# A gated feed-forward kernel: both raw products of the next unit placed ahead of a unit's last product, and the third weight sums of unit 1 moved to GpSimd

## The chip, the cores and the metric

The kernel runs on one core of a Trainium2 chip. The metric is device time in microseconds (us) of one execution; lower is better. The kernel before takes 542.69 us (median of 3 runs, 542.49 to 542.69).

Engine names as in the profile: PE is TensorE (matmul), PEld its weight loads, DVE is VectorE, ACT is ScalarE, POOL is GpSimd, SP issues DMAs.

## The reference

```python
# x: 2048 x 1024, w_gate and w_up: 1024 x 3584, w_down: 3584 x 1024, all bf16
def reference(x, w_gate, w_up, w_down):
    g = jnp.einsum("bsd,df->bsf", x, w_gate)
    u = jnp.einsum("bsd,df->bsf", x, w_up)
    h = jax.nn.gelu(g, approximate=True) * u
    return jnp.einsum("bsf,fd->bsd", h, w_down)
```

## The kernel before

The kernel multiplies 2 x 2 blocks with seven products in place of eight (a Strassen-like scheme). The rows are handled in two passes; in each pass there are 14 units, one for each 256 columns of the gate and up weights, followed by the down projection. A unit makes seven products for gate and for up, so each product is eight matmuls of 128 x 128 weights by 512 columns. Two of the seven use the bf16 inputs as they are: the raw products. The other five use sums of blocks (`s` of weights, `t` of inputs), which are kept in fp32. Unit 0 of the first pass is computed in the plain way, and unit 1 is made while the engines are still busy with that.

This is the part of a unit that the argument needs. `e`, `c` and `d` are pairs of PSUM banks, where the matmuls put their results; `hT` holds the products of gelu(gate) and up, the input of the down projection; `snap` copies a bank out with ScalarE; `keep` makes combinations of the down weights, by a ScalarE copy into a bank of the `c` pair and a VectorE subtraction, and is used only in units 2 to 13 of the first pass.

```python
def product(ps, lhs, rhs, start):
    for k in range(KH):                       # KH = 4
        matmul(ps, lhs[:, k, :], rhs[k], start and k == 0, k == KH - 1)

def first_product(e, xT, w):                  # raw (bf16)
    for i in range(2):
        product(e[i], w[:, i, :KH, :P], [xT[0][:, k, :] for k in range(KH)], True)
    return [snap(e[i], "p1") for i in range(2)]

def unit(u, banks, xT, w, s, t, p1, after_p5, aside, keep, ahead_of_p4, snap_first):
    ...
    e, c, d = banks
    for i in GU: product(c[i], w[:, i, KH:, :P], b21, True)       # second raw product
    g, up = add(c, p1)                                            # VectorE: two sums
    for i in GU: product(e[i], s["s2"][i], t["t2"], False)
    keep(0, c[0])
    g = gelu(g); times(2 * u, 0, g, up)
    u2 = [snap(e[i], "u2") for i in GU]
    keep(1, c[0]); keep(2, c[1])
    c = d
    for i in GU: product(c[i], s["s1"][i], t["t1"], True)
    p5 = [snap(c[i], "p5") for i in GU]
    after_p5()                                                    # GpSimd: next unit's s1..s4
    for i in GU: product(e[i], s["s3"][i], t["t3"], False)
    ...                                                           # sums with p5
    for i in GU: product(c[i], s["s4"][i], t["tb"], False)        # "fourth sum's product"
    ...
    ahead_of_p4()                                                 # first_product of unit u + 1
    for i in GU: product(e[i], s["sa"][i], t["t4"], False)        # last product
    times(2 * u, 1, gelu(g), up)
    times(2 * u + 1, 0, gelu(e[0]), e[1])                         # last hT multiply
# [some lines joined; branches for unit 1 and calls of `aside`, which inserts other work, cut]

def keep_part(j, part, ps):
    ...
    nc.scalar.copy(out=ps, in_=a)
    dve(made[j][:, part], ps, b, SUB)
```

Ahead of the loop, VectorE makes the weight sums of unit 1:

```python
    finish(bank[0:4], 0)
    s["s1"] += s["how"]["s1"](s, range(1, 2))
    nxt = {"p1": first_product(odd, xT, w)}
    s.make("sa", "s2", "s3", "s4")
    t.make("t1")
```

Of the kernel before, what the change touches and what calls it, by code (L numbers as in the profile page):

```python
# [10 lines left out]
def kernel(  # L11
# [26 lines left out]
    P = nc.NUM_PARTITIONS  # L38
# [13 lines left out]
    KH = NKB // 2  # L52
# [29 lines left out]
    def slot(shape, dtype, name):  # L82
        return kpool.tile(shape, dtype, name=name, tag="k")
# [3 lines left out]
    even, odd, cc, dd = bank[6:8], bank[0:2], bank[2:4], bank[4:6]  # L87
# [17 lines left out]
    def snap(ps, name):  # L105
        t = slot([P, N], f32, name)
        nc.scalar.copy(out=t, in_=ps)  # L107
        return t
# [40 lines left out]
    def sums_s(w, eng):  # L149
        GU = range(2)  # L150
        sh = [P, KH, P]
        a11, a21 = [[w[:, i, :KH, h : h + P] for i in GU] for h in (0, P)]
        a12, a22 = [[w[:, i, KH:, h : h + P] for i in GU] for h in (0, P)]
        return Sums(
            how={
                "s1": lambda q, GU=GU: [new(eng, a21[i], a22[i], ADD, "s1", sh) for i in GU],
                "s2": lambda q: [new(eng, q["s1"][i], a11[i], SUB, "s2", sh) for i in GU],
                "s3": lambda q: [new(eng, a11[i], a21[i], SUB, "s3", sh) for i in GU],
                "s4": lambda q: [new(eng, a12[i], q["s2"][i], SUB, "s4", sh) for i in GU],
                "sa": lambda q: [cast(a22[i], "sa", sh) for i in GU],  # L160
            }
        )
# [22 lines left out]
    def product(ps, lhs, rhs, start):  # L185
        for k in range(KH):
            matmul(ps, lhs[:, k, :], rhs[k], start and k == 0, k == KH - 1)

    def first_product(e, xT, w):
        for i in range(2):  # L190
            product(e[i], w[:, i, :KH, :P], [xT[0][:, k, :] for k in range(KH)], True)
        return [snap(e[i], "p1") for i in range(2)]

    def unit(u, banks, xT, w, s, t, p1, after_p5, aside, keep, ahead_of_p4, snap_first):
        GU = range(2)

        def add(ps, other):

            g = new(dve, ps[0], other[0], ADD, "sum", dtype=f32)
            dve(ps[1], ps[1], other[1], ADD)  # L200
            return g, ps[1]

        b21 = [xT[0][:, KH + k, :] for k in range(KH)]
        e, c, d = banks
        for i in GU:
            product(c[i], w[:, i, KH:, :P], b21, True)
        aside(-2)
        g, up = add(c, p1)
        aside(-1)
        for i in GU:  # L210
            product(e[i], s["s2"][i], t["t2"], False)
        aside(0)
        keep(0, c[0])
        if snap_first:
            u2 = [snap(e[i], "u2") for i in GU]
            g = gelu(g)
        else:
            g = gelu(g)
        c11 = g, up
        if not snap_first:  # L220
            times(2 * u, 0, *c11)
            u2 = [snap(e[i], "u2") for i in GU]
        keep(1, c[0])
        keep(2, c[1])
        c = d
        for i in GU:
            product(c[i], s["s1"][i], t["t1"], True)
        p5 = [snap(c[i], "p5") for i in GU]
        after_p5()
        for i in GU:  # L230
            product(e[i], s["s3"][i], t["t3"], False)
        g, up = new(dve, e[0], p5[0], ADD, "sum", dtype=f32), banks[1][not snap_first]
        dve(up, e[1], p5[1], ADD)
        if snap_first:
            times(2 * u, 0, *c11)
        for i in GU:
            product(c[i], s["s4"][i], t["tb"], False)
        times(2 * u + 1, 1, gelu(g), up)
        aside(1)
        g, up = add(c, u2)  # L240
        ahead_of_p4()
        for i in GU:
            product(e[i], s["sa"][i], t["t4"], False)
        times(2 * u, 1, gelu(g), up)
        aside(2)
        times(2 * u + 1, 0, gelu(e[0]), e[1])
# [106 lines left out]
    sa = {}  # L353
# [113 lines left out]
    xT = new_x()  # L467
# [4 lines left out]
    w = load_w(1)  # L472
# [4 lines left out]
    def plain(ps, c, kos, parts=1):  # L477
        n = N // parts
        for k in range(kos.start, kos.stop, 2):
            for part in range(parts):  # L480
                cols = slice(part * n, (part + 1) * n)
                for p, (j, i) in zip(ps, [(j, i) for j in range(2) for i in range(2)]):
                    for ko in (k, k + 1):
                        matmul(
                            p[:, cols],
                            wf[:, i, ko, j * P : (j + 1) * P],
                            xT[c][:, ko, cols],
                            ko == 0 and part == 0,
                            ko == NKB - 1,
                        )  # L490
# [6 lines left out]
    s, t = sums_s(w, dve), sums_t(xT)  # L497
    with tc.manual_schedule(engines={ENG.Activation}):
        def keep_warm(n, cols):
            for _ in range(n):  # L500
                nc.tensor.matmul(  # L501
                    bank[3][:, :cols], lhsT=warm[:, :P], rhs=warm[:, :cols], start=True, stop=True
                )

        keep_warm(NWARM, N)
        for i in range(NS):
            if i > 0:
                keep_warm(3, 2 * P)
            turn(xT, xn0, 0, i, on_act if i == 1 else on_dve)
        plain(bank[0:4], 0, range(0, 2), parts=2)  # L510
        plain(bank[0:4], 0, range(2, NKB))
        s["s1"] = s["how"]["s1"](s, range(1))
        finish(bank[0:4], 0)
        s["s1"] += s["how"]["s1"](s, range(1, 2))
        nxt = {"p1": first_product(odd, xT, w)}
        s.make("sa", "s2", "s3", "s4")
        t.make("t1")

    seen = xpool.tile([P, 1], f32, name="seen")
# [15 lines left out]
    for ip in range(NPASS):  # L535
        for u in range(1 if ip == 0 else 0, NU):
            js = making(u) if ip == 0 else []

            def prepare():
                nonlocal ahead  # L540
                if first:
                    pool_behind(t["t4"][-1])
                nxt["w"], nxt["s"] = ahead, None
                if u + 1 < NU:
                    nxt["s"] = make_s(ahead, pool)
                if u + 2 < NU:
                    ahead = load_w(u + 2)
                if len(js) == 1:
                    store_made(js[0])
                for j in js[1:]:  # L550
                    keep_whole(j)
                if ip == 0:
                    fetch_wd(making(u + 1))

            def keep(part, ps):
                if js:
                    keep_part(js[0], part, ps)

            def aside(part):
                if (ip, u) == (0, 1) and part < 0:  # L560
                    rest_of_0(part + 2)
                if part == 0 and "t4" not in t:
                    t.make("t4")

            def ahead_of_p4():
                if u + 1 < NU:
                    nxt["p1"] = first_product(even if u % 2 else odd, xT, nxt["w"])

            e = odd if u % 2 else even
            p1 = nxt.pop("p1", None) or first_product(e, xT, w)  # L570
            first = (ip, u) == (0, 1)
            with tc.manual_schedule(engines={ENG.Activation}) if first else nullcontext():
                unit(u, (e, cc, dd), xT, w, s, t, p1, prepare, aside, keep, ahead_of_p4, first)
            if u + 1 < NU:
                w, s = nxt["w"], nxt["s"]

        last = ip == NPASS - 1
        got, nxt = {}, {}

        def more(step):  # L580

            nonlocal ahead
            if last:
                return
            if step in (-1, 0, 2):
                store_made({-1: NJ - 3, 0: NJ - 2, 2: NJ - 1}[step])
            if step == 0:
                xT[:] = new_x()
            if step >= 24 and step % 2 == 0 and step // 2 - 12 < len(moves):
                c, ko = moves[step // 2 - 12]  # L590
                transposing(xT, c, ko, (2 * (ip + 1) + c) * N)
            if step == 50:
                got["w"], ahead = load_w(0), load_w(1)
            if step == 58:
                got["s"] = make_s(got["w"], dve)
            if step == 62:
                got["t"] = make_t(xT)

        down(ip, even + cc, dd + odd, last, more)
        even, odd, cc, dd = odd, even, dd, cc  # L600
        if not last:
            w, t, s = got["w"], got["t"], got["s"]
# [29 lines left out]
```

## Time and profile before

| quantity | before | where it is read |
|---|---|---|
| time, median of 3 | 542.69 us | the runs |
| span | 540.6 us | head of the page |
| PE busy | 535.9 us, 99% | page, part 1 |
| one unit, from unit 2 on | 12.60 us | starts of the fourth sum's product, timeline |
| end of the plain products to unit 1's fourth sum (end of that product's first matmul) | 6.11 us | matmul ends in the trace |

The page of the kernel before, three of its parts: engines with busy time and share, the chain that ended last, and four groups of PE (line, operation, output<-inputs, shape, count | busy us, mean ns of one | idle before).

```profile
PE 535.9 (99%) x2414; PEld 378.8 (70%) x2414; DVE 341.4 (63%) x526; ACT 258.7 (48%) x463; POOL 236.4 (44%) x213
...
PE bank L111 98%; PE bank L501 1%; PE bank L448 0%; ACT st L412 0%; DVE warm L432 0%
...
L111 PE MATMUL bank<-t,s 128*128 128x512 f32 x648 | 157.4, 398 | 0.0
...
L111 PE MATMUL bank<-xT,w 128*128 128x512 bf16 (+1 forms) x504 | 116.2, 377 | 0.0
...
L111 PE MATMUL bank<-t,sa 128*128 128x512 f32 x216 | 58.6, 413 | 0.0
...
L111 PE MATMUL bank<-tb,s 128*128 128x512 f32 x216 | 53.3, 389 | 0.0
```

TensorE is the limit, and it is almost always fed. The group names tell the products: `xT,w` raw, `t,s` the three from sums of both sides, `tb,s` the fourth sum's, `t,sa` the last. Their means differ although all do the same size: 389 ns where an fp32 product follows another, 413 ns for the last product, which stands between two raw ones. Matmuls overlap, so these means are not the time that each adds; for that one compares the ends of consecutive matmuls. The Trainium skill, "Perfetto Trace Analysis", section on the tensor engine instruction, says that these ends are computed from the instruction's size, not observed. A single distance is therefore modelled; summed over a unit, the distances agree with the starts (12.60 us from 319.66 to 332.26 below).

The order of the products in one unit of the second pass, from the timeline of PE of the kernel before (start us, length us, instructions):

```profile
319.66 1.98 PE L111 MATMUL bank<-tb,s 128*128 128x512 f32 x8
321.48 1.90 PE L111 MATMUL bank<-xT,w 128*128 128x512 bf16 x8
323.03 2.19 PE L111 MATMUL bank<-t,sa 128*128 128x512 f32 x8
325.06 1.90 PE L111 MATMUL bank<-xT,w 128*128 128x512 bf16 x8
326.61 5.82 PE L111 MATMUL bank<-t,s 128*128 128x512 f32 x24
332.26 1.98 PE L111 MATMUL bank<-tb,s 128*128 128x512 f32 x8
```

Type changes twice each way per unit. From 319.66 to 332.26 is 12.60 us. The distance in ns of each matmul's end from the end of the one before, in that unit, worked out from the trace:

```
tb,s  227 227 226 227 227 226 227 226
xT,w  232 215 216 216 216 216 215 216
t,sa  228 226 230 236 227 234 231 226
xT,w  232 215 216 216 216 216 215 216
t,s   228 226 230 235 228 234 231 227 226 227 227 226 ... (then 227, 227, 226 to the end)
```

A bf16 matmul adds 215.7 ns, an fp32 one 226.6. The first bf16 matmul after fp32 adds 232, and the first eight fp32 matmuls after bf16 add about 25 ns too much together.

The list of PEld's waits of the kernel before (who waited <- for what: us in all, times, longest). "issue" means no producer was found:

```profile
PEld L111 <- issue: 14.0, 53, 0.3
...
PEld bank L111 <- DVE t L90: 0.3, 1, 0.3
PEld bank L111 <- DVE hT L90: 0.3, 1, 0.3
```

The 53 waits are the changes from fp32 to bf16. The two waits for VectorE are the only real stalls after the start, both in unit 1.

### The profile page before, as it was taken

The numbers are of one execution on the slowest core, as the hardware profiler recorded it, in microseconds if no ns is written. First come the engines' busy times: TensorE is split into PE (matmuls) and PEld (weight loads), VectorE is DVE, ScalarE is ACT, GpSimd is POOL, SyncE is SP. The second block draws the span as 40 slices with busy tenths as digits, with TensorE's granted clock in tenths as the row PEclk, the third lists the DMA queues.
The fourth block names the chain that finished last, engine by engine and source line by source line (L and its number), as shares of the span: only waits on it lengthen the run. The fifth ranks groups of instructions, "written<-read, shape, count | busy, mean of one in ns | idle before, by whom it ended". The sixth has DMA issues, their size and how long they took to land.

```text
span 540.6 us, 7439 instructions
## 1 busy us (share of the span) xinstructions
PE 535.9 (99%) x2414; PEld 378.8 (70%) x2414; DVE 341.4 (63%) x526; ACT 258.7 (48%) x463; POOL 236.4 (44%) x213
## 2 busy tenths in 40 slices
PE   9999999999999999999999999999999999999997
PEld 5567777667766646888876776677777775488885
DVE  2986666776666895694945545555544559676730
ACT  2566666566665410255355555555555541114431
POOL 0069966677774400000097777777766600000000
PEclk9999999999999999999999999999999999999999
DMA  9776666666654899979672222222331069363751
GB/s 245 152 187 176 175 183 203 190 185 199 200 165 171 269 381 313 295 189 294 230 194 79 78 79 78 79 78 80 84 100 50 1 196 384 140 236 95 231 188 49
DMA packets 108133, 93.28 MB, mean 173 GB/s; under 512 B 17216, under 2 KB 92992, under 8 KB 108096
## 3 DMA queue, kind: packets, MB, share of 16 engines
q1 hardware_dynamic: 108096, 92.82, 59.2%
q8 instruction: 19, 0.31, 0.3%
q14 instruction: 18, 0.15, 0.1%
HBM read 74.45 MB, written 15.20 MB: 166 GB/s over the span
## 4 chain that ended last, share of the span: by engine, by line
PE 99%; ACT 0%; DVE 0%; issue 0%
PE bank L111 98%; PE bank L501 1%; PE bank L448 0%; ACT st L412 0%; DVE warm L432 0%
## 5 line engine op out<-in xcount | busy, mean ns | idle before, releaser
L93 POOL TENSOR_TENSOR s<-w 128x512 fp32r<-128x512 bf16 x100 | 116.9, 1189 | 154.9 <-PE bank L111 154.9
L111 PE MATMUL bank<-t,s 128*128 128x512 f32 x648 | 157.4, 398 | 0.0
L111 PEld LDWEIGHTS bank<-t,s 128*128 128x128 f32 x648 | 121.6, 188 | 28.2 <-DVE t L90 0.3
L111 PE MATMUL bank<-xT,w 128*128 128x512 bf16 (+1 forms) x504 | 116.2, 377 | 0.0
L107 ACT COPY p<-bank 128x512 f32<-128x512 f32 x124 | 70.5, 591 | 94.0 <-PE bank L111 94.0
L90 DVE TENSOR_TENSOR hT<-g,bank 128x512 bf16<-128x512 f32 x112 | 76.6, 687 | 55.1 <-ACT g L179 49.5
L111 PEld LDWEIGHTS <-w 128*128 128x128 bf16 x504 | 45.1, 98 | 59.0 <-issue 13.4
L90 DVE TENSOR_TENSOR sum<-bank,p 128x512 f32<-128x512 f32 x54 | 37.4, 692 | 52.6 <-PE bank L111 50.9
L179 ACT ACTIVATE g<-sum 128x512 f32<-128x512 f32 x81 | 51.5, 636 | 34.5 <-DVE sum L90 33.6
L111 PE MATMUL bank<-q 128*128 128x512 f32 x240 | 58.9, 389 | 0.0
L111 PE MATMUL bank<-t,sa 128*128 128x512 f32 x216 | 58.6, 413 | 0.0
L93 POOL TENSOR_TENSOR s<-w,s 128x512 fp32r<-128x512 bf16 x50 | 57.7, 1175 | 0.0
L93 POOL TENSOR_TENSOR s<-s,w 128x512 fp32r<-128x512 f32 x50 | 57.0, 1161 | 0.0
L111 PE MATMUL bank<-tb,s 128*128 128x512 f32 x216 | 53.3, 389 | 0.0
L111 PEld LDWEIGHTS bank<-q 128*128 128x128 f32 x240 | 45.1, 188 | 9.3
L111 PE MATMUL bank<-raw,hT 128*128 128x512 bf16 x224 | 48.7, 379 | 0.0
L111 PEld LDWEIGHTS bank<-t,sa 128*128 128x128 f32 x216 | 40.7, 188 | 10.6
L111 PEld LDWEIGHTS bank<-tb,s 128*128 128x128 f32 x216 | 40.6, 188 | 8.4
L102 ACT CAST tb<-raw 128x512 fp32r<-128x512 bf16 x28 | 17.2, 626 | 59.6 <-DMA raw<-in_w_down_dram 24.2
L107 ACT COPY u<-bank 128x512 f32<-128x512 f32 x62 | 35.9, 590 | 19.7 <-PE bank L111 19.7
L90 DVE TENSOR_TENSOR bank<-bank,p 128x512 f32<-128x512 f32 x54 | 37.8, 700 | 8.9 <-PE bank L111 5.8
L90 DVE TENSOR_TENSOR q<-hT 128x512 fp32r<-128x512 bf16 x56 | 38.5, 687 | 4.7 <-PE bank L111 4.7
(45 smaller groups left out, 444.7 us busy)
## 6 DMA issues: line engine op xcount, KB each, us to landing
raw<-in_w_down_dram SPq DMA_DIRECT2D x80, 256.0 KB, 4.8
q<-td SPq DMA_DIRECT2D x60, 256.0 KB, 5.0
w<-in_w_gate_dram SPq DMA_DIRECT2D x27, 512.0 KB, 5.9
w<-in_w_up_dram SPq DMA_DIRECT2D x27, 512.0 KB, 7.0
td<-m SPq DMA_DIRECT2D x12, 768.0 KB, 4.6
w<-td SPq DMA_DIRECT2D x6, 1024.0 KB, 9.5
out_dram<-st SPq DMA_DIRECT2D x32, 128.0 KB, 1.7
td<-w SPq DMA_DIRECT2D x2, 768.0 KB, 7.0
```

The costliest lines, as they stand in the source:

```text
L90: nc.vector.tensor_tensor(out=out, in0=a, in1=b, op=op)
L93: nc.gpsimd.tensor_tensor(out=out, in0=a, in1=b, op=op)
L102: nc.scalar.copy(out=t, in_=src)
L107: nc.scalar.copy(out=t, in_=ps)
L111: nc.tensor.matmul(ps, lhsT=lhs, rhs=rhs, start=start, stop=stop, skip_group_check=True)
L179: nc.scalar.activation(g, src, ACT.Gelu_apprx_tanh)
L501: nc.tensor.matmul(bank[3][:, :cols], lhsT=warm[:, :P], rhs=warm[:, :cols], start=True, stop=True)
```

## The change

Its intent, as far as the diff tells: one raw product moves next to the other, ahead of the last product, so that the type changes once each way per unit; and VectorE, which limits unit 1, is relieved of two operations. `e`, `c` and the sums are the same; no matmul is added or removed.

```diff
-    def first_product(e, xT, w):
+    def raw_products(e, c, xT, w):
         for i in range(2):
             product(e[i], w[:, i, :KH, :P], [xT[0][:, k, :] for k in range(KH)], True)
-        return [snap(e[i], "p1") for i in range(2)]
+        p1 = [snap(e[i], "p1") for i in range(2)]
+        for i in range(2):
+            b21 = [xT[0][:, KH + k, :] for k in range(KH)]
+            product(c[i], w[:, i, KH:, :P], b21, True)
+        return p1
@@ unit
-        b21 = [xT[0][:, KH + k, :] for k in range(KH)]
         e, c, d = banks
-        for i in GU:
-            product(c[i], w[:, i, KH:, :P], b21, True)
@@ ahead of the loop
+        s["s3"] = sums_s(w, pool)["how"]["s3"](s)
         s["s1"] = s["how"]["s1"](s, range(1))
         ...
-        nxt = {"p1": first_product(odd, xT, w)}
-        s.make("sa", "s2", "s3", "s4")
+        nxt = {"p1": raw_products(odd, cc, xT, w)}
+        s.make("sa", "s2", "s4")
@@ the two calls of first_product in the loop become raw_products(e, cc, xT, w)
```

More of the change, by code (lines that the diff above doesn't have):

```diff
@@ L566, in ahead_of_p4 @@
                 if u + 1 < NU:
-                    nxt["p1"] = first_product(even if u % 2 else odd, xT, nxt["w"])
+                    nxt["p1"] = raw_products(
+                        even if u % 2 else odd, cc, xT, nxt["w"]
+                    )
             e = odd if u % 2 else even
-            p1 = nxt.pop("p1", None) or first_product(e, xT, w)
+            p1 = nxt.pop("p1", None) or raw_products(e, cc, xT, w)
             first = (ip, u) == (0, 1)
```

## The prediction

> **What bounds it.** TensorE. The page has PE busy 99% of 540.6 us, granted clock 1.0; the chain of waits is 98% the matmul line. Listing consecutive matmul ends, after 9 us only two gaps are stalls: 382 ns at 27.5 us and 419 ns at 29.2 us, against a steady 227. Both fall in unit 1, where VectorE works without pause from 21.8 to 31.5 us (timeline); the wait list names "DVE hT" and "DVE t". From 30 us on PE never waits: each unit takes 12.60 us. Only the spacing of matmuls is left.
>
> **What a boundary costs.** A unit runs fp32 x32, raw (bf16) x8, fp32 x8, raw x8 (timeline). End-to-end spacing is 216 ns for bf16, 226.6 for fp32. The first bf16 after fp32 takes 232 (16 lost). An fp32 run after a bf16 run starts 227, 226, 231, 234, 228, 235, 230, 226: some 25 ns more than products that don't follow bf16. (Weight loads take 98 ns bf16, 188 fp32. The Trainium skill, "TensorE: Matmul & The Clock Gate", section on weight-path perf modes, gives fast weight load to non-FP32 input, which agrees; that the hand-over refills this path is my guess.) One round trip costs an estimated 41 ns.
>
> **What the change does.** Matmul work is equal. 25 times (12 in the first pass, 13 in the second) the second raw product joins the first, ahead of the last product: one round trip fewer per unit, 25 x 0.041 = 1.0 us, all critical. Unit time should fall from 12.60 to 12.56 us.
>
> The two third-sum operations of unit 1 leave VectorE (pitch 0.6 us, 1.3 us together) for an idle GpSimd (1.19 us each elsewhere; ready near 14.5 us, needed after 28). VectorE then meets the transposed input's last landing (22.8 us), so an estimated 0.7 us survives. That should remove both unit-1 stalls: 0.35 us, and 0.05 of restart. It also frees, in time, the bank with unit 1's second up-value, which the earlier raw product now overwrites.
>
> **What it risks.** The next unit's first sum now follows the last hT multiply on VectorE, some 1.4 us later than before. In pass 0 ScalarE then runs keep, gelu, two u2 copies, two keeps and p5 back to back (pitches 0.48 to 0.53 us). By these, p5 ends within 0.05 us of when the fourth sum's first weight load wants its bank; before, it had 1.0 us of slack. Possible stall 0 to 0.1 us in each of 12 units; the second pass has no keeps and ample slack. I allow 0.2 us in all. GpSimd's buffers shift too, but its new wait on the last product has over 2 us of slack.
>
> **Sum.** -1.0 -0.4 +0.2 = -1.2 us: 541.4 us, range 540.7 to 542.3. Chances: faster by over 2% 0.01, within 2% 0.98, slower by over 2% 0.01.
>
> **What would show it.** Right: raw matmuls x16 and fp32 x40 in the timeline; weight-load waits on "issue" falling from 53 to about 28; 12.56 us per unit; the last product keeping its slow 413 ns mean while the first fp32 product gets faster; no stall near 27 and 29 us; pass-0 p5 copies ending close to the start of the fourth sum's product. Wrong: PE gaps once per pass-0 unit before that product, or before unit 1's second raw product; or unit time unchanged, because the slow start belongs to the position and not the type change.
>
> **What would make it wrong.** ScalarE or VectorE steps 0.1 us longer than read here would stall every pass-0 unit: up to +2 us, cancelling the gain.

## The result, and the profile after

| | before | after |
|---|---|---|
| time, median of 6 runs | 542.69 us (541.93 to 543.12) | 542.15 us (541.51 to 543.22) |
| span of the profiled run | 540.6 us | 539.8 us |
| unit in the second pass | 12.600 us | 12.560 us |
| unit in the first pass (units 3 to 13) | 12.600 us | 12.58 to 12.634 us |
| end of the plain products to unit 1's fourth sum | 6.11 us | 5.68 us |

The ratio of the times is 0.9993, with a 95% interval of 0.9979 to 1.0006: the same. (Ratios here are the mean time of one kernel's fast runs over that of the other's of the same rounds, so not quite the ratio of the medians.) Two further sets of five runs gave 0.9983 (0.9970 to 0.9995) and 0.9985 (0.9972 to 0.9997). By these ratios the change is a gain of 0.4 to 0.9 us, where 1.2 us were predicted; the first set alone does not exclude no gain at all.

The same parts of the page after:

```profile
PE 535.1 (99%) x2414; PEld 379.5 (70%) x2414; DVE 334.9 (62%) x524; ACT 255.4 (47%) x463; POOL 239.2 (44%) x215
...
L111 PE MATMUL bank<-t,s 128*128 128x512 f32 x648 | 151.7, 390 | 0.0
...
L111 PE MATMUL bank<-xT,w 128*128 128x512 bf16 (+1 forms) x504 | 111.9, 376 | 0.0
...
L111 PE MATMUL bank<-t,sa 128*128 128x512 f32 x216 | 58.8, 414 | 0.0
...
L111 PE MATMUL bank<-tb,s 128*128 128x512 f32 x216 | 54.0, 392 | 0.0
```

The `t,s` products lost the slow start (398 to 390 ns), the last product kept it (414). The fourth sum's product became a little slower (389 to 392): that is where the gain leaks away. PEld's waits of the changed kernel show it too:

```profile
PEld L111 <- issue: 7.4, 28, 0.3
PEld bank L111 <- issue: 2.0, 12, 0.2
```

The type changes fell from 53 to 28 as planned, the two waits for VectorE are gone, and twelve new ones have come up; the page's groups put them in the fourth sum's product. They are one in each of units 2 to 13 of the first pass. What the end of unit 1's stalls is worth shows in the timeline of its first three fp32 products, the first line before, the second after:

```profile
24.35 6.22 PE L111 MATMUL bank<-t,s 128*128 128x512 f32 x24
24.20 5.80 PE L111 MATMUL bank<-t,s 128*128 128x512 f32 x24
```

The timeline of PE after, second pass, for comparison with the one of before; the line of the first product begins where the window cuts it:

```profile
321.08 3.63 PE L111 MATMUL bank<-xT,w 128*128 128x512 bf16 x16
324.35 2.19 PE L111 MATMUL bank<-t,sa 128*128 128x512 f32 x8
326.38 5.60 PE L111 MATMUL bank<-t,s 128*128 128x512 f32 x24
331.82 1.97 PE L111 MATMUL bank<-tb,s 128*128 128x512 f32 x8
```

Three `t,s` products now take 5.60 us in place of 5.82, since they follow fp32. In the first pass the distances of matmul ends around the new wait, in unit 8 (trace, ns), beside the same product in the second pass:

```
first pass,  tb,s  249 236 236 234 226 230 235 227   (sum 1873)
second pass, tb,s  227 226 227 227 226 227 227 225   (sum 1812)
```

Only 22 ns of this is a visible gap, but the seven matmuls after it are spaced more widely, and together the late start costs 61 ns.

What it waits for is seen in VectorE, ScalarE and the weight loads of unit 8. Before (timeline, lines of three engines; the last product had ended at 111.58 us and the second raw product at 113.32):

```profile
111.68 0.69 DVE L90 TENSOR_TENSOR hT<-g,bank 128x512 bf16<-128x512 f32 x1
112.49 0.69 DVE L90 TENSOR_TENSOR sum<-bank,p 128x512 f32<-128x512 f32 x1
...
113.22 0.59 ACT L273 CAST bank<-raw 128x512 f32<-128x512 bf16 x1 [1.78 <-DVE sum L90]
...
115.73 1.11 ACT L273 CAST bank<-raw 128x512 f32<-128x512 bf16 x2
116.77 1.08 ACT L107 COPY p<-bank 128x512 f32<-128x512 f32 x2
...
118.40 1.09 PEld L111 LDWEIGHTS bank<-tb,s 128*128 128x128 f32 x5
```

After:

```profile
112.93 0.69 DVE L90 TENSOR_TENSOR hT<-g,bank 128x512 bf16<-128x512 f32 x1 [1.75 <-PE bank L111]
113.54 0.68 DVE L90 TENSOR_TENSOR sum<-bank,p 128x512 f32<-128x512 f32 x1
...
114.25 0.59 ACT L274 CAST bank<-raw 128x512 f32<-128x512 bf16 x1 [1.71 <-DVE sum L90]
114.78 0.63 ACT L179 ACTIVATE g<-sum 128x512 f32<-128x512 f32 x1
115.31 1.06 ACT L107 COPY u<-bank 128x512 f32<-128x512 f32 x2
116.25 1.12 ACT L274 CAST bank<-raw 128x512 f32<-128x512 bf16 x2
117.30 1.08 ACT L107 COPY p<-bank 128x512 f32<-128x512 f32 x2
...
118.00 1.01 PEld L111 LDWEIGHTS bank<-tb,s 128*128 128x128 f32 x5 [0.17 <-issue]
```

The first of the two `p` copies frees the bank that the fourth sum's product writes. Before, it starts at 116.77 and ends at 117.36, 1.04 us ahead of the weight load at 118.40. After, it starts at 117.30 and ends at 117.89, and the weight load follows at 118.00; it wanted to start at 117.88 (as in the version e3 below). The chain is: last product, last hT multiply, first sum, keep copy, gelu, two `u` copies, two keep copies, first `p` copy. Before, the second raw product came after the last product: the sum started at 112.49, just after the first half of that raw product (112.45), and the last hT multiply had ended by then (112.37).

Because the timed runs scatter, the sums below use profile times from the end of the plain products (bf16, unit 0) to the last matmul. Before: 512.43 us; after, in three profiles: 511.78, 511.63, 511.55 us.

| part | before | after, three profiles |
|---|---|---|
| plain products to unit 1's fourth sum | 6.11 | 5.68, 5.71, 5.69 |
| twelve units of the first pass | 151.20 | 151.45, 151.27, 151.21 |
| unit 13 to unit 0 of the second pass (down projection) | 100.24 | 100.29, 100.29, 100.29 |
| thirteen units of the second pass | 163.80 | 163.28, 163.28, 163.28 |
| to the last matmul | 91.08 | 91.08, 91.08, 91.08 |

### The profile page after: what moved, and what is told of

It is laid out like the page before. It is cut to its first block, busy times and chain, and to the rows that moved or that the text cites. A ratio compares the mean times of both kernels' runs of the same rounds, so it can differ in the third digit from the quotient of the medians.

```text
span 539.8 us, 7428 instructions
## 1 busy us (share of the span) xinstructions
PE 535.1 (99%) x2414; PEld 379.5 (70%) x2414; DVE 334.9 (62%) x524; ACT 255.4 (47%) x463; POOL 239.2 (44%) x215
## 4 chain that ended last, share of the span: by engine, by line
PE 99%; ACT 0%; DVE 0%; issue 0%
PE bank L111 98%; PE bank L502 1%; PE bank L449 0%; ACT st L413 0%; DVE warm L433 0%
## 5 line engine op out<-in xcount | busy, mean ns | idle before, releaser
L93 POOL TENSOR_TENSOR s<-w 128x512 fp32r<-128x512 bf16 x102 | 120.0, 1198 | 165.1 <-DVE t L90 86.7
L111 PE MATMUL bank<-t,s 128*128 128x512 f32 x648 | 151.7, 390 | 0.0
L111 PE MATMUL bank<-xT,w 128*128 128x512 bf16 (+1 forms) x504 | 111.9, 376 | 0.0
L111 PEld LDWEIGHTS <-w 128*128 128x128 bf16 x504 | 47.0, 98 | 58.5 <-issue 6.9
L111 PEld LDWEIGHTS <-hT 128*128 128x128 bf16 x224 | 21.8, 98 | 26.5 <-issue 0.5
```

Of the source, the lines that this page charges most:

```text
L93: nc.gpsimd.tensor_tensor(out=out, in0=a, in1=b, op=op)
L111: nc.tensor.matmul(ps, lhsT=lhs, rhs=rhs, start=start, stop=stop, skip_group_check=True)
```

## The experiments

The theory: (1) the gain per type change and the gain in unit 1 are as predicted, and independent; (2) the rest is lost because the first sums of the next unit now stand behind the last hT multiply, which makes a chain through VectorE and ScalarE just longer than the time that it has. Rivals: the first pass is slower because of its other work (keeps, stores, DMA), whatever the order; or the gain in unit 1 was an accident of one execution's landing times; or the slow start of fp32 runs belongs to a product's place rather than to the change of type.

All twelve runs gave correct outputs.

### The changed kernel, again

No edit.

> The changed kernel once more, so that the others can be compared on one chip. Its profile gave 12.56 us per unit in the second pass and 12.633 in units 3 to 13 of the first, where one gap per unit stands before the fourth sum's product. Theory: the same again to 0.01 us, as everything after the start is set by instruction order. Profile span 0.5 to 1.1 us under the kernel before; the timed runs scatter by over 1 us, so their ratio should be 0.998 to 1.000. Rival (the pass-0 gap is a chance of one execution): units of the first pass at 12.56 this time.

Measured: 541.96 us (median of 5), ratio to before 0.9983. Second pass 12.560 us in every unit; first pass 12.577 to 12.634, with the visible gap in six of the units 3 to 13 only. In units without it the fourth sum's product still begins slowly (241, 233, 230 ns in one such unit, then 227). The weight load waits in these units too: in all three profiles it starts 0.113 to 0.115 us after the end of the first `p` copy in each of units 2 to 13, some 0.13 us later than the run of weight loads before it would have brought it. So every unit is held up by about the same time; what reaches the matmuls differs (21 to 61 ns in this product), and why it differs is not shown. That is less constant than I expected to 0.01 us, but it is no chance of one execution.

> The changed kernel a third time, beside the version with the sums ahead, to compare them in the same rounds. Expected: 12.56 us per unit in the second pass; 12.58 to 12.64 in the first; ratio to the kernel before about 0.9985.

Measured: 541.92 us, ratio 0.9985; 12.560 us in the second pass and 12.577 to 12.621 in the first.

### One part of the change at a time

`e1`: the kernel before, plus

```diff
+        s["s3"] = sums_s(w, pool)["how"]["s3"](s)
         s["s1"] = s["how"]["s1"](s, range(1))
...
-        s.make("sa", "s2", "s3", "s4")
+        s.make("sa", "s2", "s4")
```

> The kernel before, with only unit 1's third weight sums moved to GpSimd. Theory: both unit-1 stalls vanish; from the end of the plain products to the start of unit 1's fourth sum's product it takes 5.68 us in place of 6.11, that is 0.4 us less; every later unit stays at 12.60. Total about 0.4 us less than before. Rival (the start gained for another reason, such as the landing times of that execution): the step stays near 6.1 us.

Measured: plain products to unit 1's fourth sum 5.70 us; every unit 12.600; plain products to the last matmul 512.02 us, that is 0.41 less than before. Both waits for VectorE are gone from the list. The ratio of the timed runs, 0.9996 (0.9982 to 1.0010), can't resolve 0.4 us. The rival falls.

`e2`: the changed kernel with this edit undone.

> The changed kernel, with the third weight sums back on VectorE. Theory: the step from the plain products to unit 1's fourth sum stays at 6.1 us with both stalls; 12.56 us per unit in the second pass, 12.633 in the first from unit 3 on; in unit 1 the earlier raw product may wait up to 0.1 us for the bank that VectorE still reads. Total 0.1 to 0.4 us less than before. If the two parts need each other, unit 1 shows a new gap over 0.2 us before the second raw product.

Measured: 6.11 us to unit 1's fourth sum, with gaps of 389 and 423 ns, much as before (382 and 419); 12.56 us per unit in the second pass and 12.63 in eleven of the first pass's twelve; no gap before unit 1's second raw product, so the two parts don't need each other there. The total was not usable: this execution's down projection waited for DMA (100.99 us in place of 100.29; two matmul distances of 581 and 598 ns near 207 us, put down to the landing of `w_down`). Its median, 542.91 us, and ratio, 0.9996, are therefore no evidence against 12.56 us.

### The chain, taken away

`e3`: the changed kernel, with the next unit's two first sums moved ahead of the last hT multiply. They need only the raw products, which are done by then.

```diff
-        g, up = add(c, p1)
+        g, up = sums or add(c, p1)
...
             def aside(part):
+                if part == 2 and u + 1 < NU:
+                    nxt["sums"] = add(cc, nxt["p1"])
```

`aside(2)` stands just before the last hT multiply; `unit` takes `nxt.pop("sums", None)`.

> The changed kernel, with the next unit's first two sums on VectorE put ahead of the last hT multiply of a unit, so that they no longer wait for the last product. Theory (the first-pass gap is the chain last product, hT, sum, keep, gelu, copies, p5 on VectorE and ScalarE): ScalarE's p5 copies end about 1 us before the fourth sum's weight load wants them, no gap in the first pass, 12.56 us in both passes, 0.8 us less than the changed kernel, 1.6 less than before. Rival (the first pass is slower because of its stores, keeps and DMA traffic whatever the order): the units of the first pass stay at 12.63.

Measured: 541.31 us, ratio to before 0.9974 (0.9961 to 0.9986); 12.56 us in every unit of both passes; plain products to the last matmul 511.03 us, 1.40 less than before and 0.52 to 0.75 less than the changed kernel. The timeline of unit 8:

```profile
112.93 0.69 DVE L90 TENSOR_TENSOR hT<-g,bank 128x512 bf16<-128x512 f32 x1 [0.54 <-PE bank L111]
...
115.16 1.11 ACT L273 CAST bank<-raw 128x512 f32<-128x512 bf16 x2
116.20 1.08 ACT L107 COPY p<-bank 128x512 f32<-128x512 f32 x2
...
117.88 1.09 PEld L111 LDWEIGHTS bank<-tb,s 128*128 128x128 f32 x5
```

The last hT multiply stands where it stood in the changed kernel (112.93 us), but the `p` copy starts at 116.20 instead of 117.30, and the weight load is not held up. All other work of the first pass is unchanged, so the rival of "other work" falls. By its profile this version beats both kernels; the timed runs show its lead over the kernel before, but their scatter covers that over the changed kernel.

> The version with the next unit's first sums ahead of the last hT multiply, again, beside the changed kernel. Expected: 12.56 us in every unit, 0.5 to 0.9 us less than the changed kernel by the profile, ratio to the kernel before about 0.997.

Measured in the same rounds as the third set of the changed kernel: 541.18 us against 541.92, ratio to before 0.9967 (0.9953 to 0.9981), again 12.56 us in every unit and 511.03 us. Comparing the means of the five runs of each, this version is 0.50 us faster than the changed kernel in the first set (541.58 against 542.09) and 0.77 in the second (541.23 against 542.00); the profiles say 0.52 to 0.75.

### The chain, made longer

An extra ScalarE copy of the same data into the same bank, in each keep:

```diff
         nc.scalar.copy(out=ps, in_=a)
+        if part == 2:
+            nc.scalar.copy(out=ps, in_=a)
         dve(made[j][:, part], ps, b, SUB)
```

> The changed kernel with one more ScalarE copy of 0.52 us pitch in each keep, ahead of the p5 copies of the first pass (it writes the same values again). Theory (the gap before the fourth sum's product is the VectorE and ScalarE chain from the last product): each of units 3 to 13 grows by about the pitch, from at most 12.633 to about 13.1 us, 5 to 6 us in all; the second pass stays at 12.56. Rival (other traffic of the first pass): units grow by under 0.1 us.

Measured (one look): 542.19 us; first pass about 12.70 us, second 12.56. A miss: 13.1 was expected, and taken alone this growth of 0.07 us fits the rival. The timeline showed why: the scheduler had put the copy behind the first `p` copy, so only the second one came later, by 0.50 us. By an estimate from the weight loads of unit 8 in the changed kernel, that one had some 0.3 us to spare (it ended at 118.38; the weight load that needs its bank came at 118.83, less the 0.11 us of the release), and accordingly the gap moved to the second half of the fourth sum's product (298 to 326 ns instead of 227). The dose was not where it was meant to be.

> The same extra ScalarE copy in the kernel before, where the p5 copies ended 1.0 us ahead of the weight load that waits for them. Theory: the slack takes it, every unit stays at 12.60 us, total within 0.1 us. Rival (ScalarE's own load, not the chain behind the last product, sets the first pass): units of the first pass grow as in the dose on the changed kernel.

Measured (one look): 542.50 us and 12.60 us in every unit. The kernel before has room for the copy; but here too it stood behind the first `p` copy, so this tests only the slack of the second.

`e8` puts the dose ahead of both `p` copies (`part == 1` in the edit above), which the built order confirmed before the run.

> The changed kernel with the extra ScalarE copy of about 0.5 us in another place: the scheduler had put the first dose behind the first p5 copy, this one stands ahead of both (seen in the built order). Theory: the first p5 copy ends 0.5 us later, so the gap before the fourth sum's product grows by about as much: 13.0 to 13.15 us in units 3 to 13 of the first pass in place of 12.59 to 12.63, 12.56 in the second, total 5 to 6 us more than the changed kernel. Rival (other traffic of the first pass): under 12.7.

Measured (one look): 548.21 us; units 3 to 13 at 13.11 to 13.135 us, second pass 12.56. PEld's waits and the weight load of unit 8:

```profile
PEld bank L111 <- issue: 7.5, 11, 0.7
...
121.51 1.08 ACT L107 COPY p<-bank 128x512 f32<-128x512 f32 x2
...
122.22 0.76 PEld L111 LDWEIGHTS bank<-tb,s 128*128 128x128 f32 x4 [0.68 <-issue]
```

The copy added 0.50 us to ScalarE and 0.50 us to each unit (13.13 against 12.63): one for one, as a chain without slack demands. In the trace the first `p` copy ends at 122.11, 0.11 us before the weight load, as in the changed kernel.

`e9` puts the same dose into the version with the sums ahead.

> The same extra copy ahead of p5, in the version with the next unit's first sums ahead of the last hT multiply. Theory: there p5 ends about 1 us early, so the slack takes the dose: 12.56 us per unit in both passes, total as that version without the dose. Rival: units of the first pass grow by 0.3 us or more.

Measured (one look): 541.96 us, and 12.56 us in every unit; plain products to last matmul 511.01 us. The slack took the dose: in unit 8 the first `p` copy ends 1.09 us before the weight load in `e3` and still 0.57 us before it here. With `e3` and `e8` this settles that the chain causes the wait.

### A shorter chain by another way

`e6`: the first keep is made by VectorE straight from SBUF, without ScalarE and PSUM.

```diff
+        if part == 0:
+            dve(made[j][:, 0], a, b, SUB)
+            return
         nc.scalar.copy(out=ps, in_=a)
```

> The changed kernel, with the first keep made by VectorE straight from its two SBUF tiles, without the ScalarE copy through PSUM. The chain behind the last product loses one ScalarE step of 0.52 us. Theory: the gap before the fourth sum's product goes, first pass at 12.56 us, about 0.8 us less than the changed kernel. If VectorE, with two inputs from SBUF, and GpSimd get in each other's way, one of the two gets longer than 0.69 and 1.19 us per instruction, and the gap may come back elsewhere.

Measured: 541.28 and 541.34 us in two runs, 548.40 and 549.27 in two others; ratio 1.0024 (0.9949 to 1.0100). The gap did go: units 5 to 13 took 12.56 to 12.62 us. But the subtraction, 0.69 us with one input in PSUM, took about 1.30 us in ten units and 0.90 in one, and in unit 3 of the profiled run (one of the two slow ones) this happened:

```profile
51.40 2.31 POOL L93 TENSOR_TENSOR s<-s,w 128x512 fp32r<-128x512 f32 x2
51.96 6.75 DVE L90 TENSOR_TENSOR m<-raw 128x512 fp32r<-128x512 bf16 x1
53.64 2.30 POOL L93 TENSOR_TENSOR s<-w 128x512 fp32r<-128x512 bf16 x2
55.88 2.29 POOL L93 TENSOR_TENSOR s<-w,s 128x512 fp32r<-128x512 bf16 x2
```

The VectorE instruction lasted 6.75 us, and ended only after GpSimd's series, which ended at 58.17. PE then stood for 5.1 us (the wait list; matmul end to matmul end it was 5.87 us) and the next matmuls came 427 ns apart. The Trainium skill, "GPSIMD Engine Reference", section Specifications, says that GpSimd shares its SBUF interfaces with VectorE, with contention where a VectorE instruction has two SBUF inputs. This agrees, at 1.30 to 6.75 us in place of 0.69; with two SBUF inputs and no GpSimd work beside it, a VectorE instruction of the same shape took 0.69 us too (`s<-w` at 12.00 us of the kernel before). The detour of the keeps through PSUM in the original has this use: there is no such instruction in its keeps.

### One more type change

`e7`: the changed kernel with the last product cut in two, its first half between the two raw products and the second after them.

> The changed kernel, with the last product cut in two: its first half stands between the two raw products, its second half after them. One more round trip between bf16 and fp32 per unit than in the changed kernel, but with only four fp32 matmuls in one of the runs. Theory (the slow start belongs to the change of type): second pass at 12.56 + 0.016 for the added bf16 hand-over + 0.012 to 0.025 for the added slow start, that is 12.588 to 12.601 us per unit, and the four matmuls after the first raw product show the spacing 227, 226, 231, 234. Rival (the slow start belongs to the last product's data or its place): 12.56 to 12.577.

Measured (one look): 12.607 us per unit in the second pass, that is 47 ns more than the changed kernel, where 28 to 41 were expected. The distances in one unit (ns):

```
xT,w  447 216 216 216 216 215 216   (447: a matmul's record is missing here)
t,sa  228 226 230 235
xT,w  231 216 216 216 216 215 216 216
t,sa  228 230 236 233
t,s   226 230 236 227 234 231 227 226 227 ...
```

Here a change of type cost a slow start in both places, so the rival of place falls. The second slow start is longer than usual here, some 45 ns against 25; why, I don't know. (The total, 543.65 us, also holds a wait of the down projection for DMA of 0.9 us, 101.15 against 100.29 us.)

## Why the prediction was right or wrong

- **TensorE bounds, and only matmul spacing is left: right.** PE is 99% busy in both profiles.
- **41 ns per round trip, 25 of them, 1.0 us: right.** Second pass 12.600 to 12.560 us. From unit 1's fourth sum to the last matmul the version with the sums ahead, where nothing stalls, takes 505.32 us against 506.32: 1.00 us, or 40 ns each. The signs came as named: 28 waits on "issue", 414 ns for the last product, 390 for the first ones.
- **Unit 1, 0.4 us from the move to GpSimd: right.** 0.40 to 0.43 us in the changed kernel, 0.41 alone. The feared wait for unit 1's bank did not come, even without the move.
- **The risk named: right in kind and place.** The chain, the copy at its end, the product that waits for it, the first pass only.
- **Its size: wrong, and this is the step that failed.** "Possible stall 0 to 0.1 us in each of 12 units ... I allow 0.2 us in all." The range held: the units lost 0.02 to 0.07 us each. The allowance did not. Twelve units at 12.56 us would be 150.72; they took 151.21 to 151.45, so 0.49 to 0.73 us were lost, and 0.05 more on the way into the down projection: 0.54 to 0.78 us in place of 0.2. The prediction's path was right: it had the end of the `p` copy within 0.05 us of the time at which the weight load wants the bank, and in unit 8 these were 117.89 and 117.88. Two costs were left out. The weight load followed the end of the `p` copy by 0.11 us, in every unit from 2 to 13, while the prediction took the end of the copy for the release of the bank; in the trace an entry without operands, 51 ns long, lies between them, and the built program waits there for two semaphores (ScalarE's and GpSimd's), so two waits in turn are the likely but untested cause. And a late fp32 run mostly starts slowly: 22 ns of visible gap came with 61 ns lost in ten units of the first profile, though in unit 5 the same gap cost 21 ns in all.
- **Sum.** With the measured term: -1.0 - 0.4 + 0.54 to 0.78 = -0.6 to -0.9 us; the profiles say -0.65, -0.80 and -0.88. The first comparison of timed runs, 0.54 us in the medians, was inside the stated range of 540.7 to 542.3, which says little: the six runs of the changed kernel alone spread from 541.51 to 543.22, wider than the range. Executions differ by more than the gain: in the profiles, the last transpose of the start ended between 6.74 and 8.16 us, and two of them show down projections that waited 0.7 to 0.9 us for DMA. I had not allowed for this in the reading of a gain of 1.2 us from six runs.
- **Open.** Why an interrupted fp32 run needs about eight matmuls to get back to 226.6 ns is not settled. The prediction's guess, a refill of the weight-load path, has one fact beside it: bf16 weight loads take 98 ns and fp32 ones 188. The Trainium skill, "TensorE: Matmul & The Clock Gate", section on weight-path perf modes, gives fast weight load to input that is not FP32, in agreement. But a similar slow start follows a wait within fp32 (249, 236, 236, 234), so it is not the type change alone.

## What to carry to other kernels

When the limiting engine has no gaps left, look at the distances between its instructions by kind, and group work of a type together; here that was worth 40 ns for each pair of type changes. When a product is moved, list what was ordered behind it on the other engines: a sum that used to run in the shadow of another product can come to stand behind a multiply, and a slack of 1 us can be gone with no engine busier than before; moving the sum back ahead of the multiply took the loss away. Treat a chain whose end meets its deadline as a stall in every round (here the release took another 0.11 us, and all twelve units waited), with the cost of the restart added to the wait.

## What the Trainium skill lacked or had wrong

- "TensorE: Matmul & The Clock Gate" has no cost of a change between bf16 and fp32 matmuls: 16 ns for the first bf16 one and about 25 ns over the first eight fp32 ones, 40 ns per round trip.
- The same page, section on the back-to-back issue gap, gives about 131 ns per matmul for a sustained stream of pairs at N=512, and N/2.4 + 2.5 (216 ns) for an isolated one. Here a long stream of pairs of weight load and bf16 matmul ran at 215.7 ns each, and the measurement decides; another part of the page, on the 56 ns gap, has 215.7 ns for back-to-back matmuls at N=512, which agrees. The page has no figure for fp32 streams, which ran at 226.6.
- No page has the slow restart after a late release: 61 ns lost where the gap itself is 22 ns, in ten of twelve units of one profile.
- No page gives the time from the end of a ScalarE copy to a TensorE weight load that waits for it together with a second semaphore: 0.11 us here.
- No page has a VectorE instruction held up through a whole series of GpSimd instructions: one with two SBUF inputs took 6.75 us, until after the sixth of the GpSimd instructions beside it, where 0.69 us is its time with one input in PSUM and about 1.30 us was the rule beside GpSimd. This belongs to "GPSIMD Engine Reference", which names the contention but has no such figure.
